# Windowed attention and two expert layers on one core: order and buffers of the first loads, casts of the weights

## The chip, the cores and the metric

The kernel runs on one core of one Trainium2 chip. The metric is the device time of an execution in microseconds (us), as the median of several runs. One core has TensorE (PE, which multiplies matrices), VectorE (DVE), ScalarE (ACT), GpSimd (POOL) and SyncE (SP); here SyncE issues all the transfers between HBM and the core's SBUF. Matrix products are written to PSUM, which has eight banks here, shared out over three rings.

## The reference

```python
# q, k, v: (4, 8, 576, 64)
scores = (q @ k.transpose(0, 1, 3, 2)) / sqrt(64)
rel = pos[:, None] - pos[None, :]
scores = where((rel >= 0) & (rel < 64), scores, -1e9)
attn = exp(scores - max(scores)); attn /= sum(attn) + 1e-9
x = (attn @ v)                       # to (2304 tokens, 512)
h = maximum(x @ w_in, 0);  x = (h * h) @ w_out          # d_ff = 2048
h = x @ w2_in;             out = (h * cos(h)) @ w2_out  # d_ff = 2048
```

The weights reach the kernel as 64-bit floating point numbers, read as pairs of 32-bit words, and are converted on the chip. Products are made in float32 split into a high and a low part (three products for one).

## The kernel before

**Staging.** The 2304 tokens are cut into nine attention units n of 256 tokens, each in two groups g of heads. `attention(n, g, key, sp, ...)` loads qk (576 KB) and v (512 KB), makes the scores S on TensorE (`scores`, L451), takes the masked maximum on VectorE (`neg_max`, L463), the exponential on ScalarE (`exp`, L469), sums and normalises on VectorE (L475 to L479), transposes on TensorE (T, L487), copies the result to PT, multiplies by v on TensorE (O, L501), and writes the high part of X on ScalarE (L535) and the low part on VectorE (L538). Scores, T and O of a group pass through one ring of PSUM banks: "acc" (four banks) for group (0,0), "at" (two banks) for all others. qk, v, pb and PT have one buffer each for all the groups.

**Weights.** w1 has 16 blocks j. `convert_w` loads the raw words of a block (1024 KB, L271) into one of 17 weight buffers "W", scales both words on ScalarE (L241, two instructions), shifts, merges and adds on VectorE (L294, L297, L302), casts the result to the high part in a second buffer (`c5`, L241 on ScalarE or L245 on VectorE) and subtracts for the low part (L323, VectorE). The raw buffer is free after that. The load of block j waits for the low part of block j - 4. Blocks of w2 are converted in the same way later and stored to HBM.

**Products.** `units` are UnitA (first layer; units 0, 1 and 2 of 256 tokens, then pairs of 512) and UnitB (second layer, 384 tokens). `items` is the list of (unit, j) in TensorE's order. For each item `g1` makes the first product ph (12 matmuls, L814), ScalarE and VectorE make g from it (L578 to L591), and `g2` makes the second product accA (12 matmuls, L605) LAG = 2 items later. g1 and g2 are tied in a line by `line`. Unit 0 is alone for the first SK = 4 blocks; then its items alternate with those of unit 1:

```python
SK = 4
items = [(units[0], j) for j in range(SK)]
for j in range(NJ - SK):
    items += [(units[0], SK + j), (units[1], j)]
```

**Order.** Every step is an `op` with the engines that may do it and a cost for each, a key, what it depends on, and the buffers it takes and uses. `Plan.run` walks through time: of the ops that can start within 0.03 us of the earliest it takes the one with the lowest key, on the engine that would end it first. What comes out is a fixed order on each engine; on the chip each engine takes its instructions in that order and waits for what each needs. A transfer costs SyncE 0.6 us in the plan and lands 1.6 us plus its bytes at 250 GB/s later. The first calls are

```python
for g in range(NG):
    attention(0, g, -60.0 + 8.0 * g, 4.0)
for j in range(NJ):
    convert_w(w1, j, (-12.0) + 3.0 * (j if j < SK else 2 * j - SK),
              w_lo[j - 4][1] if j >= 4 else None, early=(-60.0) + 4.0 * j if j < 3 else None)
```

Of the kernel before, what the change touches and what calls it, by code (L numbers as in the profile page):

```python
# [85 lines left out]
class Plan:  # L86
# [6 lines left out]
    def op(self, engs, key, fn, deps=(), take=(), use=(), lat=None):  # L93
        if lat is None:
            lat = self.PE_LAT if "PE" in engs else self.LAT
        o = Op(engs, key, fn, [d for d in deps if d is not None], list(take), lat)
        o.seq = len(self.ops)
        self.ops.append(o)
        for b in (*take, *use):
            b.users.append(o)  # L100
        return o
# [61 lines left out]
def act_us(n, sbuf=True):  # L163
    return 0.05 + 0.093 * sbuf + n / 1200.0
# [15 lines left out]
def kernel(  # L180
# [24 lines left out]
    NUA = NT // UA  # L205
    NUB = NT // UB
    HB = UA // P
    LAG = 2

    psum = bass.MemoryType.PSUM  # L210
# [20 lines left out]
    X = cp.tile([P, 2, NCC, 4 * UA], F32R, name="X")  # L231

    def dma(key, fn, nbytes, deps=(), take=(), use=(), n=1, order=()):
        return op({"SP": 0.6 * n}, key, fn, [*deps, *order], take, use, lat=1.6 + nbytes / 250e3)

    def eng_of(e):
        return {"DVE": nc.vector, "POOL": nc.gpsimd}[e]
# [22 lines left out]
    def convert_w(src, j, key, after=None, dst=None, early=None):  # L260

        nm = f"{src.tensor.name}_{j}"
        raw, rb = {}, R["W"].buf()
        wb = R["W"].buf() if dst is None else None

        def ld(e):
            raw["t"] = wp.tile([P, 2, DM, 2], I32, tag=f"W{rb.slot}", name=f"raw_{nm}")  # L270
            nc.sync.dma_start(  # L271
                raw["t"].rearrange("p a n two -> p (a n two)"), src[j].bitcast(I32))

        o_ld = dma(key - 3 if early is None else early, ld, P * 2 * DM * 8, [after], [rb])

        def words():
            t = raw["t"].rearrange("p a n two -> p (a n) two")
            return t[:, :, 0], t[:, :, 1]

        def c0(e):  # L280
            hw = words()[1].bitcast(F32)
            copy(e, hw, hw, 2.0**-112)

        def c1(e):
            lw = words()[0]
            copy(e, lw, lw.bitcast(U32), 2.0**-29)

        o0 = op({"ACT": act_us(2 * DM)}, key, c0, [o_ld], use=[rb])
        o1 = op({"ACT": act_us(2 * DM)}, key, c1, [o_ld], use=[rb])
        s, tb = {}, R["w"].buf()  # L290

        def c2(e):
            s["w"] = cv.tile([P, 2 * DM], I32, tag="w", name=f"cw_{nm}")
            nc.vector.tensor_scalar(s["w"], words()[1], 3, None, ALU.logical_shift_left)  # L294

        def c3(e):
            nc.vector.scalar_tensor_tensor(  # L297
                s["w"], words()[1], -(1 << 31), s["w"], ALU.bitwise_and, ALU.bitwise_or)

        def c4(e):  # L300
            w = words()[1] if dst is None else s["w"]
            nc.vector.tensor_tensor(w, s["w"], words()[0], ALU.add)  # L302

        def w32():
            if dst is None:
                return raw["t"].bitcast(F32)[:, :, :, 1]
            return s["w"].bitcast(F32).rearrange("p (a n) -> p a n", a=2)

        o2 = op({"DVE": dve_us(2 * DM, True)}, key, c2, [o0], [tb], use=[rb])
        o3 = op({"DVE": dve_us(2 * DM)}, key, c3, [o2], use=[rb, tb])  # L310
        o4 = op({"DVE": dve_us(2 * DM) + 0.3}, key, c4, [o3, o1], use=[rb, tb])
        if dst is None:
            tb = rb
        if dst is not None:
            return [dma(key, lambda e: nc.sync.dma_start(dst[j], w32()), P * 2 * DM * 4, [o4],
                        use=[tb])]

        def c5(e):
            new_w(wb, nm)
            copy(e, wb.tile[:, :, 0], w32())  # L320

        def c6(e):
            nc.vector.tensor_tensor(  # L323
                wb.tile[:, :, 1], w32(), f32(wb.tile[:, :, 0]), ALU.subtract)

        hi = op({"ACT": act_us(2 * DM), "DVE": dve_us(2 * DM, True) + 0.3}, key, c5, [o4],
                [wb], [tb])
        lo = op({"DVE": dve_us(2 * DM)}, key, c6, [hi], use=[tb, wb])
        w_hi[j] = [hi, hi]
        w_lo[j] = [lo, lo]  # L330
        w_buf[j] = wb
# [75 lines left out]

    x_hi = {}
    x_lo = {}
    loads = []  # L410
    turns = {"acc": None, "at": None}

    spans = [(0, 1), (1, 1), (2, 1)] + [(n, 2) for n in range(3, NUA, 2)]
    x_col = [0, UA, 2 * UA] + [((n - 3) % 4) * UA for n in range(3, NUA)]
# [1 line left out]
        [m for m in range(n) if x_col[m] == x_col[n]][-1:] for n in range(NUA)]  # L416
    g1_last = {}

    def attention(n, g, key, sp):

        nm = f"{n}_{g}"
        t = {}
        ring = "acc" if n == 0 and g == 0 else "at"
        pool = ps_acc if ring == "acc" else ps_at
        qb, vb, pbuf, smb, ptb = (R[x].buf() for x in ("qk", "v", "pb", "sm", "PT"))
        sb = [R[ring].buf() for _ in range(2)]
        tb = [R[ring].buf() for _ in range(2)]
        ob = R[ring].buf()

        def load_qk(e):  # L430
            t["qk"] = ap_.tile([P, 2, QK], F32, tag="qk", name=f"qk_{nm}")
            nc.sync.dma_start(t["qk"], qk[n, g])

        def load_v(e):
            t["v"] = ap_.tile([P, NR, 4, D], F32, tag="v", name=f"v_{nm}")
            nc.sync.dma_start(t["v"], v[n, g])

        l0 = dma(key - 3, load_qk, P * 2 * QK * 4, [], [qb], order=loads[-1:])
        l1 = dma(key - 2, load_v, P * NR * 4 * D * 4, [], [vb], order=[l0])
        loads.append(l1)  # L440

        def scores(eng):
            t["pb"] = ap_.tile([P, 2, 2, HB, P], F32, tag="pb", name=f"pb_{nm}")
            S = t["S"] = [
                pool.tile([P, 2, HB, P], F32, tag=ring, name=f"S_{nm}_{e}") for e in range(2)]
            for r in range(2):
                for i in range(HB):
                    for e in range(2):
                        for c in range(2):
                            q0 = (2 * i + c) * WINDOW  # L450
                            nc.tensor.matmul(  # L451
                                S[e][HALF[c], r, i], t["qk"][HALF[e], r, q0:q0 + WINDOW],
                                t["qk"][HALF[e], r, UA + q0:UA + q0 + P],
                                start=(r == 0 and i == 0), stop=(r == 1 and i == HB - 1),
                                skip_group_check=True)

        o_s = op({"PE": 0.35 + 8 * 0.104}, key, scores, [l0, turns[ring]], [*sb, pbuf], [qb])

        def neg_max(eng, e, r, i):
            if e == 0 and r == 0 and i == 0:  # L460
# [27 lines left out]

        def p_copy(eng, e):
            if e == 0:  # L490
                t["pt"] = ap_.tile([P, 2, 2, UA], F32, tag="PT", name=f"PT_{nm}")
            copy(eng, t["pt"][:, e].rearrange("p r q -> p (r q)"),
                 t["T", e].rearrange("p r i q -> p (r i q)"))

# [13 lines left out]
        for e in range(2):  # L508
            k_e = key + e * sp
            ex = []  # L510
            for r in range(2):
                for i in range(HB):
                    first = prev is None
                    prev = op({"DVE": 0.36}, k_e, lambda q, e=e, r=r, i=i: neg_max(q, e, r, i),
                              [o_s, o_mask[mask_kind(HB * n + i)], prev],
                              [smb] if first else [],
                              [sb[e], pbuf] + ([] if first else [smb]))
                    ex.append(op({"ACT": 0.59}, k_e, lambda q, e=e, r=r, i=i: exp(q, e, r, i),
                                 [prev], use=[pbuf, smb]))
            o_r = op({"DVE": 0.33}, k_e, lambda q, e=e: recip(q, e), ex, use=[smb])  # L520
            o_n = op({"DVE": dve_us(512)}, k_e, lambda q, e=e: norm(q, e), [o_r], use=[smb, pbuf])
            o_t = op({"PE": 4 * pe_us(P)}, k_e, lambda q, e=e: transp(q, e),
                     [o_n, o_setup], [tb[e]], [pbuf])
            o_pt = op({"ACT": act_us(512, False), "DVE": dve_us(512)}, k_e,
                      lambda q, e=e: p_copy(q, e), [o_t, o_pt],
                      [] if e else [ptb], [tb[e]] + ([ptb] if e else []))
            o_p.append(o_pt)
        o_v = op({"PE": 0.35 + 16 * 0.053}, key + sp, weighted, [l1, *o_p], [ob], [ptb, vb])
        turns[ring] = o_v
# [250 lines left out]

    units = [UnitA(n, k) for n, k in spans] + [UnitB(n) for n in range(NUB)]
    NSA = len(spans)
    SK = 4
    items = [(units[0], j) for j in range(SK)]
    for j in range(NJ - SK):
        items += [(units[0], SK + j), (units[1], j)]
# [57 lines left out]

    cv = ctx.enter_context(tc.tile_pool(name="cv", bufs=1))
    for g in range(NG):
        attention(0, g, -60.0 + 8.0 * g, 4.0)
    for j in range(NJ):
        convert_w(w1, j, (-12.0) + 3.0 * (j if j < SK else 2 * j - SK), w_lo[j - 4][1] if j >= 4 else None, early=(-60.0) + 4.0 * j if j < 3 else None)
    w2_done = {}  # L850
    gs = {}

    def att_key(n, g):
        if n == 1:
            return -40.0 + 8.0 * g, 4.0
        if n <= 4:
            return 16.0 + 8.0 * (n - 2) + 4.0 * g, 2.0
        s = 3 + (n - 5) // 2
        return s * NJ + 6.0 * ((n - 5) % 2) + 3.0 * g, 1.5
# [97 lines left out]
```

## Time and profile before

| what | value |
|---|---|
| median of 3 runs | 917.96 us (915.41 to 918.77) |
| profiled execution | 918.24 us |
| its span, first to last instruction | 916.4 us |
| mean granted TensorE clock | 0.989 |
| busy: PE, DVE, ACT | 881.4, 570.4, 469.1 us |

The profile shows one execution. A row of the timeline gives start, duration, engine, source line, operation, output and inputs and the number of instructions merged, and in brackets how long the engine stood idle before it and who ended that. Busy shares of TensorE say that it has work, not that it works at its peak: at a granted clock of 0.5 the same matmuls take twice as long.

### The profile page before, as it was taken

How to read it: one execution, taken by the hardware profiler on the slowest of the kernel's cores; microseconds unless marked ns; L12 is line 12 of the kernel's file. 1: busy time of each engine (PE TensorE's matmuls, PEld its weight loads, DVE VectorE, ACT ScalarE, POOL GpSimd, SP SyncE). 2: the span in 40 equal slices, each digit the busy share in tenths (PEclk: the TensorE clock that was granted, in tenths of full speed). 3: DMA queues.
4: the chain of work that ended last, by engine and by line, in shares of the span. 5: the costliest groups of instructions: out<-in, count | busy, mean ns of one | idle time of the engine just before them, and what ended most of it. 6: DMA issues, size and time to landing. Idle time of an engine off the chain costs nothing.

```text
span 916.4 us, 14455 instructions
## 1 busy us (share of the span) xinstructions
PE 881.4 (96%) x5616; PEld 777.3 (85%) x5616; DVE 570.4 (62%) x1307; ACT 469.1 (51%) x1007; POOL 5.0 (1%) x25
## 2 busy tenths in 40 slices
PE   3689899999999999999999999999999999999998
PEld 2579899998888878887888999898989999898987
DVE  4999886544544355534444976766766766866664
ACT  5878757666655566644433543433443433433433
POOL 2000000000000000000000000000000000000000
PEclk9799999999999999999999999999999999999999
DMA  6565315433444254323342200200200200200000
GB/s 266 228 221 218 131 61 167 163 122 119 153 153 141 70 187 156 127 95 124 124 175 92 73 9 1 66 5 1 69 1 1 70 1 1 70 1 1 35 1 35
DMA packets 23749, 85.47 MB, mean 93 GB/s; under 512 B 2433, under 2 KB 7041, under 8 KB 19585
## 3 DMA queue, kind: packets, MB, share of 16 engines
q1 hardware_dynamic: 23680, 84.55, 26.4%
q8 instruction: 44, 0.72, 0.3%
q14 instruction: 25, 0.20, 0.1%
HBM read 66.72 MB, written 17.83 MB: 92 GB/s over the span
## 4 chain that ended last, share of the span: by engine, by line
PE 92%; DVE 3%; DMA 2%; ACT 1%; issue 1%; ACTq 0%; DVEq 0%
PE ph L814 44%; PE accB L747 22%; PE accA L605 21%; PE S L451 2%; PE O L501 2%; DMA qk<-in_qk_dram 2%; PE T L487 1%; DMA x_dram<-x 1%; DVE W_in_w_dram L323 1%; DVE cw_in_w_dram L297 1%; DVE cw_in_w_dram L294 0%; DVE pb L479 0%; DVE X L538 0%; ACT g L582 0%; ACT r L586 0%
## 5 line engine op out<-in xcount | busy, mean ns | idle before, releaser
L814 PE MATMUL ph<-X,W_in_w_dram 128*128 128x256 f32 (+1 forms) x1152 | 225.4, 344 | 5.0 <-DVE W_in_w_dram L323 3.4
L605 PE MATMUL accA<-g,W_in_w_dram 128*128 128x256 f32 (+1 forms) x1152 | 223.2, 340 | 2.0 <-ACT x L625 1.6
L814 PE MATMUL ph<-X,W 128*128 128x384 f32 x1152 | 218.0, 337 | 0.0
L747 PE MATMUL accB<-W,gb 128*128 128x512 f32 x864 | 216.4, 395 | 0.0
L814 PEld LDWEIGHTS ph<-X,W 128*128 128x128 f32 x1152 | 205.2, 188 | 8.6
L814 PEld LDWEIGHTS ph<-X,W_in_w_dram 128*128 128x128 f32 x1152 | 182.8, 193 | 31.5 <-DVE W_in_w_dram L323 4.0
L605 PEld LDWEIGHTS accA<-g,W_in_w_dram 128*128 128x128 f32 x1152 | 180.5, 191 | 25.8 <-ACT x L625 2.5
L747 PEld LDWEIGHTS accB<-W,gb 128*128 128x128 f32 x864 | 161.0, 188 | 30.5
L698 ACT ACTIVATE u<-ph,quarter 128x384 f32<-128x384 f32 x96 | 55.7, 581 | 151.4 <-PE ph L814 151.4
L591 DVE TENSOR_TENSOR g<-r,g 128x256 fp32r<-128x256 f32 (+1 forms) x96 | 53.3, 556 | 103.0 <-ACT r L586 102.2
L702 DVE TENSOR_SCALAR u<-u 128x384 f32<-128x384 f32 x96 | 34.5, 359 | 109.4 <-ACT u L698 109.4
L582 ACT ACTIVATE g<-r 128x256 fp32r<-128x256 f32 (+1 forms) x96 | 50.3, 524 | 97.8 <-PE accA L605 96.4
L724 ACT ACTIVATE gb<-rr 128x384 fp32r<-128x384 f32 x96 | 50.5, 526 | 87.5 <-DVE rr L720 86.8
L578 ACT ACTIVATE r<-ph 128x256 f32<-128x256 f32 (+1 forms) x96 | 46.6, 486 | 55.3 <-PE ph L814 54.4
L241 ACT ACTIVATE raw_in_w_dram<-raw_in_w_dram 128x1024 f32<-128x1024 f32 x64 | 71.5, 1148 | 1.4 <-DMA raw_in_w_dram<-in_w_dram 1.4
L469 ACT ACTIVATE pb<-pb,mm 128x128 f32<-128x128 f32 x144 | 55.9, 391 | 11.2 <-DVE mm L463 11.2
L717 ACT ACTIVATE u<-rr,hpi 128x384 f32<-128x384 f32 x96 | 58.5, 609 | 0.3 <-DVE rr L713 0.3
L720 DVE TENSOR_TENSOR rr<-ph,u 128x384 f32<-128x384 f32 x96 | 52.9, 551 | 4.7 <-ACT u L717 4.7
L706 DVE SCALAR_TENSOR_TENSOR rr<-u,ph 128x384 f32<-128x384 f32 x96 | 53.1, 553 | 3.0
L727 DVE TENSOR_TENSOR gb<-rr,gb 128x384 fp32r<-128x384 f32 x96 | 53.0, 552 | 0.6 <-ACT gb L724 0.6
L710 DVE SCALAR_TENSOR_TENSOR rr<-u,rr 128x384 f32<-128x384 f32 x96 | 52.8, 550 | 0.6
L586 ACT ACTIVATE r<-r 128x256 f32<-128x256 f32 (+1 forms) x94 | 49.1, 523 | 2.9
(58 smaller groups left out, 540.4 us busy)
## 6 DMA issues: line engine op xcount, KB each, us to landing
raw_in_w_dram<-in_w_dram SPq DMA_DIRECT2D x32, 1024.0 KB, 6.3
qk<-in_qk_dram SPq DMA_DIRECT2D x18, 576.0 KB, 4.0
v<-in_v_dram SPq DMA_DIRECT2D x18, 512.0 KB, 3.7
w_dram<-cw_in_w_dram SPq DMA_DIRECT2D x16, 512.0 KB, 3.0
w<-w_dram SPq DMA_DIRECT2D x8, 1024.0 KB, 4.9
x_dram<-x SPq DMA_DIRECT2D x18, 256.0 KB, 2.2
xr<-x_dram SPq DMA_DIRECT2D x24, 192.0 KB, 2.4
out_dram<-o SPq DMA_DIRECT2D x18, 256.0 KB, 2.1
```

Of the source, the lines that this page charges most:

```text
L241: nc.scalar.activation(o, i, AF.Copy, scale=scale)
L469: nc.scalar.activation(t["pb"][:, e, r, i], t["pb"][:, e, r, i], AF.Exp, bias=t["mm"][:, e, r, i:i + 1], scale=-1.0, accum_out=t["sm"][:, ...
L591: nc.vector.tensor_tensor(t["g"][:, 1], t["r"], f32(t["g"][:, 0]), ALU.subtract)
L605: nc.tensor.matmul(self.acc[i][:, k, :], w[:, 1, wl, m * P:m * P + P], t["g"][:, gl, :], start=(j == 0 and p == 0 and k == 0), stop=(j == ...
L698: nc.scalar.activation(t["u"], ph()[:, 0:UB], AF.Identity, bias=quarter, scale=INV_2PI)
L706: nc.vector.scalar_tensor_tensor(t["r"], t["u"], -C1, ph()[:, 0:UB], ALU.mult, ALU.add)
L710: nc.vector.scalar_tensor_tensor(t["r"], t["u"], -C2, t["r"], ALU.mult, ALU.add)
L717: nc.scalar.activation(t["u"], t["r"], AF.Sin, bias=hpi)
L720: nc.vector.tensor_tensor(t["r"], ph()[:, 0:UB], t["u"], ALU.mult)
L727: nc.vector.tensor_tensor(t["g"][:, 1], t["r"], f32(t["g"][:, 0]), ALU.subtract)
L747: nc.tensor.matmul(self.acc[m], t["g"][:, gl, m * P:m * P + P], w[:, 1, wl], start=(j == 0 and k == 0), stop=(j == NJ - 1 and k == 2))
L814: nc.tensor.matmul(t["ph"][:, 0:u.w], wb.tile[:, 0, wl, c * P:c * P + P], u.x(xl, c), start=(c == 0 and k == 0), stop=(c == NCC - 1 and k ...
```

## The change

At the beginning the loads of qk of both groups of unit 0 get the lowest keys (-99, -98), ahead of the first weight blocks (-96, -94.5), and v of both groups -97 and -95.5. The dependency that put each group's load behind the loads of the group before (`loads`) is removed. The second groups of units 0 and 1 (`guest`) take three of the weight buffers in place of the single qk, v, pb and PT buffers, through a helper `room`, and group (0,1) uses the two banks of the "ph" ring. SK becomes 2, and the keys of the weight conversions change. `c5`, the cast of a weight block's high part, is allowed on ScalarE alone. In the planner a transfer now occupies SyncE for its bytes at 360 GB/s (at least 0.6 us) and lands 2.2 us after that, and an extra 0.3 us on `c4` is dropped.

```diff
+    A0, A1 = 2.0, -40.0
     def dma(key, fn, nbytes, deps=(), take=(), use=(), n=1, order=()):
-        return op({"SP": 0.6 * n}, key, fn, [*deps, *order], take, use, lat=1.6 + nbytes / 250e3)
+        return op({"SP": max(0.6 * n, nbytes / 360e3)}, key, fn, [*deps, *order], take, use, lat=2.2)
...
-        o4 = op({"DVE": dve_us(2 * DM) + 0.3}, key, c4, [o3, o1], use=[rb, tb])
+        o4 = op({"DVE": dve_us(2 * DM)}, key, c4, [o3, o1], use=[rb, tb])
...
-        hi = op({"ACT": act_us(2 * DM), "DVE": dve_us(2 * DM, True) + 0.3}, key, c5, [o4],
-                [wb], [tb])
+        hi = op({"ACT": act_us(2 * DM)}, key, c5, [o4], [wb], [tb])
...
-    loads = []
-    turns = {"acc": None, "at": None}
+    turns = {"acc": None, "ph": None, "at": None}
...
-    def attention(n, g, key, sp):
+    def attention(n, g, key, sp, early=None):
...
-        ring = "acc" if n == 0 and g == 0 else "at"
-        pool = ps_acc if ring == "acc" else ps_at
-        qb, vb, pbuf, smb, ptb = (R[x].buf() for x in ("qk", "v", "pb", "sm", "PT"))
+        ring = {(0, 0): "acc", (0, 1): "ph"}.get((n, g), "at")
+        pool = {"acc": ps_acc, "ph": ps_ph, "at": ps_at}[ring]
+        smb = R["sm"].buf()
+
+        guest = n < 2 and g == 1
+        if guest:
+            qb, vb, ptb = (R["W"].buf() for _ in range(3))
+            pbuf = ptb
+        else:
+            qb, vb, pbuf, ptb = (R[x].buf() for x in ("qk", "v", "pb", "PT"))
+
+        def room(name, buf, at, shape):
+            if not guest:
+                return ap_.tile([P, *shape], F32, tag=name, name=f"{name}_{nm}")
+            if at == 0:
+                t[buf] = wp.tile([P, 4 * DM], F32, tag=f"W{buf.slot}", name=f"{name}_{nm}")
+            size = math.prod(shape)
+            flat = t[buf][:, at:at + size]
+            dims = " ".join("abcd"[:len(shape)])
+            return flat.rearrange(
+                f"p ({dims}) -> p {dims}", **dict(zip("abcd", shape)))
...
-        l0 = dma(key - 3, load_qk, P * 2 * QK * 4, [], [qb], order=loads[-1:])
-        l1 = dma(key - 2, load_v, P * NR * 4 * D * 4, [], [vb], order=[l0])
-        loads.append(l1)
+        k_qk, k_v = early or (key - 3, key - 2)
+        l0 = dma(k_qk, load_qk, P * 2 * QK * 4, [], [qb])
+        l1 = dma(k_v, load_v, P * NR * 4 * D * 4, [], [vb], order=[l0])
...
-                      [] if e else [ptb], [tb[e]] + ([ptb] if e else []))
+                      [] if e or guest else [ptb],
+                      [tb[e]] + ([ptb] if e or guest else []))
...
-    SK = 4
+    SK = 2
...
-        attention(0, g, -60.0 + 8.0 * g, 4.0)
+        attention(0, g, -60.0 + A0 * g, 4.0, (-99.0 + g, -97.0 + 1.5 * g))
...
-        convert_w(w1, j, (-12.0) + 3.0 * (j if j < SK else 2 * j - SK), w_lo[j - 4][1] if j >= 4 else None, early=(-60.0) + 4.0 * j if j < 3 else None)
+        convert_w(w1, j, -6.0 + 2.0 * (j if j < SK else 2 * j - SK), w_lo[j - 4][1] if j >= 4 else None, early=-96.0 + 1.5 * j if j < 2 else None)
...
-            return -40.0 + 8.0 * g, 4.0
+            return A1 + 8.0 * g, 4.0
```

The tiles of qk, v, pb and PT are made by `room` in the places where `ap_.tile` made them.

## Rows read from the trace of the kernel before

**Rows 1.** The page's first part: busy us, share of the span, instructions.

```profile
PE 881.4 (96%) x5616; PEld 777.3 (85%) x5616; DVE 570.4 (62%) x1307; ACT 469.1 (51%) x1007; POOL 5.0 (1%) x25
```

**Rows 2.** Busy time of each engine by stretch; then granted clock, DMA share, GB/s.

```profile
0.00:21.50 21.50, 7.85 (x104) 6.24 (x104) 8.66 (x36) 10.70 (x25) 4.99 (x25) 1.00 0.69 275
21.50:60.10 38.60, 28.00 (x280) 23.79 (x281) 35.33 (x88) 31.41 (x82) 0.00 (x0) 0.82 0.56 210
60.10:125.00 64.90, 59.55 (x562) 57.38 (x561) 59.03 (x108) 49.09 (x109) 0.00 (x0) 0.97 0.44 165
125.00:420.00 295.00, 295.00 (x2285) 254.33 (x2285) 148.11 (x405) 179.42 (x436) 0.00 (x0) 1.00 0.39 132
420.00:436.00 16.00, 14.09 (x54) 10.63 (x53) 4.93 (x8) 5.54 (x10) 0.00 (x0) 0.89 0.47 173
```

**Rows 3.** SyncE's queue, timeline of its first issues.

```profile
0.73 0.37 SPq L432 DMA_DIRECT2D qk<-in_qk_dram  x1
1.16 2.18 SPq L271 DMA_DIRECT2D raw_in_w_dram<-in_w_dram  x4
3.38 0.47 SPq L436 DMA_DIRECT2D v<-in_v_dram  x1
6.63 0.33 SPq L432 DMA_DIRECT2D qk<-in_qk_dram  x1
```

**Rows 4.** The chain that ended last, first 125 us: start, us, what.

```profile
0.73 3.79 DMA qk<-in_qk_dram
...
6.63 10.51 DMA qk<-in_qk_dram
...
67.33 1.44 PE accA L605 x12
```

**Rows 5.** TensorE's timeline, parts of the first 62 us.

```profile
17.19 1.99 PE L451 MATMUL S<-qk 64*64 64x128 f32 x32 [3.15 <-DMA qk<-in_qk_dram]
19.10 1.78 PE L501 MATMUL O<-PT,v 128*64 128x64 f32 x32
...
33.53 1.97 PE L451 MATMUL S<-qk 64*64 64x128 f32 x28 [1.01 <-DVE X L538]
35.42 4.43 PE L814 MATMUL ph<-X,W_in_w_dram 128*128 128x256 f32 x27
...
46.60 1.09 PE L451 MATMUL S<-qk 64*64 64x128 f32 x28 [1.05 <-DVE X L538]
...
60.11 1.60 PE L814 MATMUL ph<-X,W_in_w_dram 128*128 128x256 f32 x12
```

**Rows 6.** VectorE's timeline, the X subtractions of groups (1,0) and (1,1).

```profile
45.85 0.69 DVE L538 TENSOR_TENSOR X<-O,X 128x512 fp32r<-128x512 f32 x1
...
58.66 0.69 DVE L538 TENSOR_TENSOR X<-O,X 128x512 fp32r<-128x512 f32 x1 [1.05 <-ACT X L535]
```

**Rows 7.** Groups of instructions from 60.1 to 125, shapes apart: busy us, mean ns.

```profile
L297 DVE SCALAR_TENSOR_TENSOR cw_in_w_dram<-raw_in_w_dram,cw_in_w_dram 128x1024 int32<-128x1024 int32 x10 | 12.2, 1225 | 0.3
L302 DVE CUSTOM_DVE_ANT_0 raw_in_w_dram<-raw_in_w_dram,cw_in_w_dram 128x2048 uint16<-128x2048 uint16 x10 | 12.2, 1222 | 0.1
L323 DVE TENSOR_TENSOR W_in_w_dram<-raw_in_w_dram,W_in_w_dram 128x1024 fp32r<-128x1024 f32 x9 | 11.0, 1221 | 0.3 <-ACT W_in_w_dram L241 0.2
...
L591 DVE TENSOR_TENSOR g<-r,g 128x256 fp32r<-128x256 f32 x17 | 7.2, 422 | 4.4 <-ACT r L586 4.3
...
L294 DVE TENSOR_SCALAR cw_in_w_dram<-raw_in_w_dram 128x1024 int32<-128x1024 int32 x9 | 6.2, 688 | 0.0
L245 DVE CAST W_in_w_dram<-raw_in_w_dram 128x1024 fp32r<-128x1024 f32 x6 | 4.2, 693 | 0.2
L241 ACT ACTIVATE W_in_w_dram<-raw_in_w_dram 128x1024 fp32r<-128x1024 f32 x3 | 3.5, 1158 | 1.3 <-DVE raw_in_w_dram L302 1.3
```

**Rows 8.** Who made TensorE wait after 125 us: in total, times, longest.

```profile
PE accA L605 <- ACT x L625: 1.6, 2, 0.9
```

**Rows 9.** Who made VectorE wait in the first 66 us.

```profile
DVE pb L463 <- PE S L451: 9.9, 2, 6.7
```

More of the change, by code (lines that the diff above doesn't have):

```diff
@@ L430, in load_qk @@
         def load_qk(e):
-            t["qk"] = ap_.tile([P, 2, QK], F32, tag="qk", name=f"qk_{nm}")
+            t["qk"] = room("qk", qb, 0, [2, QK])
             nc.sync.dma_start(t["qk"], qk[n, g])
         def load_v(e):
-            t["v"] = ap_.tile([P, NR, 4, D], F32, tag="v", name=f"v_{nm}")
+            t["v"] = room("v", vb, 0, [NR, 4, D])
             nc.sync.dma_start(t["v"], v[n, g])
-        l0 = dma(key - 3, load_qk, P * 2 * QK * 4, [], [qb], order=loads[-1:])
-        l1 = dma(key - 2, load_v, P * NR * 4 * D * 4, [], [vb], order=[l0])
-        loads.append(l1)
+        k_qk, k_v = early or (key - 3, key - 2)
+        l0 = dma(k_qk, load_qk, P * 2 * QK * 4, [], [qb])
+        l1 = dma(k_v, load_v, P * NR * 4 * D * 4, [], [vb], order=[l0])
         def scores(eng):
-            t["pb"] = ap_.tile([P, 2, 2, HB, P], F32, tag="pb", name=f"pb_{nm}")
+            t["pb"] = room("pb", pbuf, 0, [2, 2, HB, P])
             S = t["S"] = [
@@ L455, in scores @@
                                 skip_group_check=True)
-        o_s = op({"PE": 0.35 + 8 * 0.104}, key, scores, [l0, turns[ring]], [*sb, pbuf], [qb])
+        o_s = op({"PE": 0.35 + 8 * 0.104}, key, scores,
+                 [l0, turns[ring]], [*sb, pbuf], [qb])
         def neg_max(eng, e, r, i):
@@ L490, in p_copy @@
             if e == 0:
-                t["pt"] = ap_.tile([P, 2, 2, UA], F32, tag="PT", name=f"PT_{nm}")
+                t["pt"] = room("PT", ptb, 2 * DM, [2, 2, UA])
             copy(eng, t["pt"][:, e].rearrange("p r q -> p (r q)"),
```

## The prediction

> **What bounds the kernel now.** I read the page's busy shares first: TensorE (PE) has work 96% of the span [rows 1]. That is an average, so I cut the span into stretches [rows 2]. The reader is to see that TensorE's idle time lies at the beginning: 13.65 us before 21.5 (21.50 - 7.85), 10.6 from 21.5 to 60.1 (38.60 - 28.00), 5.35 from 60.1 to 125; none from 125 to 420 and 1.91 from 420 to 436. In the second stretch the granted clock is also 0.82 on average, so part of the work between 21.5 and 60.1 ran at 1.2 instead of 2.4 GHz. What can be won lies before 125; from there to 420 TensorE is full, and work shifted there comes out one for one at the end.
>
> Second view, SyncE's queue and the chain of waits: qk of group (0,0) is issued at 0.73, then four weight blocks, then v of (0,0), and only at 6.63 qk of group (0,1), because the one qk buffer is read until then [rows 3]. It lands 10.51 us later, at 17.14 [rows 4], since 4 x 1024 + 512 KB lie ahead of it: from 4.52, when the first qk landed, 5184 KB took 12.62 us, 421 GB/s. TensorE takes its work in order, so O of (0,0) at 19.10 stands behind S of (0,1) at 17.19 [rows 5].
>
> Third view, TensorE's timeline: the groups come one at a time. S of (1,0) starts in earnest at 33.53, S of (1,1) at 46.60 [rows 5], each after the X subtraction of the group before (45.85 for (1,0)) has freed its bank; the last, of (1,1), runs at 58.66 [rows 6], and at 60.11 the first product of unit 1 starts [rows 5]. From there TensorE alternates units 0 and 1 and is 92% busy. So my landmark is the start of that product. By the order of items and LAG = 2, five first products (items 0 to 4) and three second ones are behind it.
>
> **The change part by part.** *Loads.* By the keys I work out this order on SyncE: qk(0,0), qk(0,1), W0, v(0,0), v(0,1), W1, qk(1,0), qk(1,1), W2, then v of unit 1 and W3. The planner's costs serve me only for order. qk(0,1) then lands at 4.52 + 0.590 MB / 421 GB/s = 5.9 instead of 17.14, before S of (0,0) is through at 6.6 (from 4.56, 2.0 us long at this clock like the S at 17.19 [rows 5]). qk(1,0) has 576 + 1024 + 512 + 512 + 1024 + its own 576 KB behind the first: 4.325 MB / 421 GB/s = 10.3, so 14.8. The price is paid by the weights: W1 lands at about 13, W2 at 19, W3 behind v(1,0), which waits for O of (0,0) at 17 to 19 and holds W3 with it, at about 24. VectorE cannot use them sooner, so I cost this at nothing; without that cover it would be the 1024 KB of one block, 2.5 us.
>
> *Buffers.* Groups (0,1) and (1,1) each take three weight buffers of 17, six in all. Until the landmark W0 to W2 and up to four raw blocks are alive, 13 together: no wait. (0,1) takes the two "ph" banks, which nobody uses before the first product: no wait either, but the first product now waits until O(0,1) or T have left them; that was so by data anyway.
>
> *The landmark.* S(1,0) can start at 14.9. From S to the X subtraction's end (1,0) took 13.0 us (33.53 to 46.54) and (1,1) 12.75 (46.60 to 59.35) [rows 5, 6]. That gives 14.9 + 13.0 + 12.75 = 40.7 as the low bound. High bound: if S(1,0) is put behind O(0,1), at about 22, it is 47.8. I take 42.5, near the low end, with 1.8 us because (1,0) now shares ScalarE and VectorE with (0,1). A wait is added here: S(1,0) waits for its qk at 14.8, and O(0,0), ready soon after, stands behind it on TensorE for up to 2 us. X of unit 0 is then complete at about 23 to 24 and W0 about the same time; before, the rest of the first product began at 35.42 [rows 5].
>
> Check by VectorE's work. Up to 60.1 it was busy 8.66 + 35.33 = 44.0 us [rows 2]. At the new landmark only W0 to W2 are needed: two blocks less, 2 x (0.69 + 1.23 + 1.22 + 1.22) = 8.7; the shift of W5, already done, 0.7; the casts of three blocks, 2.1; three subtractions of g, 1.3 [rows 7]. There remain 31.2 us, which from its first instruction at 6.7 [rows 9] end at 42.5 with 87% busy; it ran at 92% from 21.5 to 60.1.
>
> *SK 4 to 2.* Unit 1's first product is item 3 instead of item 5. At the landmark TensorE will have done three first products and one second one, not five and three: four groups of 12 matmuls, 1.44 us each [rows 4], are still owed, 5.8 us. In return every weight block feeds 5.76 us of TensorE work from then on (four groups), against 4.4 us of VectorE conversion.
>
> So the landmark gains 60.1 - 42.5 - 5.8 = 11.8 us; with the bounds 13.6 and 6.5.
>
> *Casts.* From 60.1 to 125 six of nine casts were on VectorE, 0.693 each, three on ScalarE, 1.158 [rows 7]. All on ScalarE: VectorE 59.03 - 4.2 = 54.9 us, ScalarE 49.09 + 6.9 = 56.0 [rows 2, 7]. The busier of the two falls from 59.0 to 56.0, of 64.9. I let this stretch last as long as before; it cannot go below TensorE's 59.55 less about 1.9 for the clock (a mean of 0.97 is some 3.9 us at half rate), so up to 7.3 us may be won; what may be lost is the first rival's price.
> The Trainium skill (Perfetto Trace Analysis, Optimizing Scalar/DVE Operations) says that where VectorE has a faster mode it beats ScalarE, but that offloading can pay when VectorE is saturated. The rows agree on the first half (0.693 against 1.158) and VectorE is 91% busy there; by the first half alone each of the six casts would lose 0.46 us, 2.8 in all.
>
> *The planner's new load costs* (transfer time on SyncE) and the dropped 0.3 us reorder later work too. TensorE is full from 125 to 420, so I cost that at nothing. The exposed place is the 1.9 us of idle time from 420 to 436 [rows 2], most of it TensorE waiting for ScalarE's copies of accA [rows 8]; that wait could go or double: 2 us either way.
>
> **Sum.** The profiled execution took 918.24 (span 916.4 and 1.84 around it), 0.3 above the median of the runs, 917.96. 918.24 - 11.8 = 906.4, by the median 906.2.
>
> **The rivals.** *ScalarE becomes the bound.* For it: 56.0 us must fit where TensorE needs 59, and ScalarE also holds the relus that free TensorE's banks. From 21.5 to 60.1 it reached 31.41 of 38.6, 81%; if its waits keep it at 78%, the stretch takes 56.0 / 0.78 = 71.8, 6.9 more: 913. Against it: six casts are moved, not the whole block.
> *TensorE runs full after the landmark.* Each block now feeds both units from the third on, so conversion gets ahead and the 5.35 us of idle time go: about 900.
> *It does not bring unit 1 earlier*, because VectorE and ScalarE were the limit and not the queue. Then only the casts count, up to 3 us: 915 to 918. Against it: VectorE stood idle 9.9 us for S in this time, the first 6.7 among them [rows 9].
> *Slower.* SK = 2 puts unit 1's first product third in TensorE's order. If group (1,1) is not ready, nothing behind it runs, though W3 and W4 are there. The point is 60.1 - 5.8 = 54.3: an X(1,1) later than that loses, and at the old 59.35 it costs the whole 5.8 us, 924. It would take S(1,0) starting at 28 or later.
>
> **How the numbers follow.** Forecast 0.58, ScalarE 0.15, fuller TensorE 0.12, no earlier 0.07, slower 0.08. The forecast's own range is 903 to 912. The range 899.5 to 914.5 reaches to the fuller TensorE at one end and the ScalarE bound at the other, and leaves the last two out. A measurement here tells about 0.5%, 4.6 us, from no change: faster is the forecast, the third case and about half of ScalarE's, 0.77; within, the rest of that and most of "no earlier", 0.14; slower 0.09.
>
> **What would show it.** qk(0,1) landing near 6 and qk(1,0) near 15; S(1,0) near 15; the rest of the first product near 24; unit 1's first product near 42.5 with W3 just done; no cast of weights on VectorE; ScalarE's busy time in the next 65 us near 56; TensorE full about 12 us earlier, and nothing but that shift afterwards. It is wrong if S(1,0) stands behind O(0,1), if the product of unit 1 waits past 48, if conversions come slower than one in 5.8 us, or if the wait at 420 grows.

## The result and the profile after

The changed kernel takes 904.34 us (median of 4 runs, 903.26 to 905.20) against 918.28 before on the same chip: a ratio of 0.9855, 95% interval 0.9838 to 0.9873, 13.9 us less. The profiled execution took 904.37 with a span of 902.6.

First the stretches of [rows 2] in the changed kernel, same columns:

```profile
0.00:21.50 21.50, 11.58 (x146) 9.50 (x146) 9.39 (x56) 12.09 (x41) 5.03 (x25) 1.00 0.83 330
21.50:60.10 38.60, 29.82 (x297) 26.34 (x296) 36.86 (x71) 33.38 (x69) 0.00 (x0) 0.82 0.57 228
60.10:125.00 64.90, 63.76 (x597) 62.91 (x596) 58.10 (x108) 58.99 (x126) 0.00 (x0) 1.00 0.34 129
125.00:420.00 295.00, 294.72 (x2236) 251.40 (x2235) 143.97 (x402) 179.40 (x432) 0.00 (x0) 1.00 0.42 143
420.00:436.00 16.00, 16.00 (x72) 13.27 (x71) 5.42 (x7) 5.89 (x10) 0.00 (x0) 1.00 0.39 131
```

TensorE idles 9.9 us before 21.5 (13.65 before), 8.8 up to 60.1 (10.6), and only 1.1 up to 125 (5.35), at the full clock. The idle time at 420 to 436 is gone. Before 21.5 the granted clock reads 1.00, but the matmuls don't bear it out: 32 of S take 1.99 us there and 1.10 at 53.12, where the clock is full.

The timeline of SyncE's queue at the beginning, for [rows 3], and then of TensorE, for [rows 5]:

```profile
0.73 0.84 SPq L449 DMA_DIRECT2D qk<-in_qk_dram  x2
1.63 0.42 SPq L272 DMA_DIRECT2D raw_in_w_dram<-in_w_dram  x1
2.09 1.01 SPq L453 DMA_DIRECT2D v<-in_v_dram  x2
3.15 0.57 SPq L272 DMA_DIRECT2D raw_in_w_dram<-in_w_dram  x1
6.78 0.80 SPq L449 DMA_DIRECT2D qk<-in_qk_dram  x2
7.62 0.45 SPq L272 DMA_DIRECT2D raw_in_w_dram<-in_w_dram  x1
8.12 12.94 SPq L453 DMA_DIRECT2D v<-in_v_dram  x2
21.10 0.43 SPq L272 DMA_DIRECT2D raw_in_w_dram<-in_w_dram  x1
```

```profile
4.71 3.69 PE L468 MATMUL S<-qk 64*64 64x128 f32 x64 [4.71 <-DMA qk<-in_qk_dram]
...
15.79 1.08 PE L505 MATMUL T<-ident,pb 128*128 128x128 f32 x4 [2.30 <-ACT pb L487]
16.80 1.99 PE L468 MATMUL S<-qk 64*64 64x128 f32 x32
18.72 1.97 PE L519 MATMUL O<-PT,v 128*64 128x64 f32 x32
...
27.95 1.08 PE L505 MATMUL T<-ident,pb 128*128 128x128 f32 x4 [2.85 <-DVE pb L497]
...
33.97 1.99 PE L468 MATMUL S<-qk 64*64 64x128 f32 x32
...
46.18 2.70 PE L833 MATMUL ph<-X,W_in_w_dram 128*128 128x256 f32 x12
48.71 1.60 PE L624 MATMUL accA<-g,W_in_w_dram 128*128 128x256 f32 x12
50.15 1.60 PE L833 MATMUL ph<-X,W_in_w_dram 128*128 128x256 f32 x12
```

The loads are issued in the forecast order, and TensorE waits for none but the first: S of (0,0) and (0,1) are one run of 64. S of (1,0) starts at 16.8, S of (1,1) only at 33.97, and unit 1's first product, the landmark, at 50.15, behind three first products and one second.

To see where the 13.9 us lie, the start of the same matmul is compared in both timelines (before, then after): the first product of the sixth and last unit of layer one, and the last second products of the kernel:

```profile
412.24 2.88 PE L814 MATMUL ph<-X,W_in_w_dram 128*128 128x512 f32 x12
...
904.37 8.56 PE L747 MATMUL accB<-W,gb 128*128 128x512 f32 x36
```

```profile
402.30 2.88 PE L833 MATMUL ph<-X,W_in_w_dram 128*128 128x512 f32 x12
...
890.51 8.56 PE L766 MATMUL accB<-W,gb 128*128 128x512 f32 x36
```

9.94 us are won by 412, and 13.86 at the end. The other 3.92 are the stall at 420 to 436 [rows 8]: 1.91 of idle time and the slow clock behind it (0.89 on average there, 1.00 in the changed kernel).

### The profile page after: what moved, and what is told of

It is laid out like the page before. It is cut to its first block, busy times and chain, and to the rows that moved or that the text cites. A ratio compares the mean times of both kernels' runs of the same rounds, so it can differ in the third digit from the quotient of the medians.

```text
span 902.6 us, 14462 instructions
## 1 busy us (share of the span) xinstructions
PE 879.0 (97%) x5616; PEld 776.9 (86%) x5616; DVE 563.3 (62%) x1295; ACT 480.2 (53%) x1019; POOL 5.0 (1%) x25
## 4 chain that ended last, share of the span: by engine, by line
PE 91%; ACT 4%; DVE 3%; issue 1%; DMA 0%; ACTq 0%; DVEq 0%
PE ph L833 43%; PE accB L766 22%; PE accA L624 20%; PE S L468 2%; PE O L519 2%; PE T L505 2%; ACT raw_in_w_dram L242 1%; DVE cw_in_w_dram L298 1%; ACT pb L487 1%; DVE pb L481 0%; ACT g L601 0%; DVE pb L497 0%; ACT W_in_w_dram L242 0%; DMA qk<-in_qk_dram 0%; DVE W_in_w_dram L324 0%
```

## The experiments

Times are medians, each with its ratio to the kernel before measured on the same chip. Two theories are told apart. A: the early part gains because the groups, and unit 1 above all, are ready earlier. B (called C when narrowed): it gains because the blocks are converted faster than TensorE uses them up. The first runs undo one part of the changed kernel; those with one part alone put it into the kernel before.

### Undoing one part of the changed kernel

**SK.**

```diff
-    SK = 2
+    SK = 4
```

> The changed kernel with SK = 4 again (the keys of the conversions follow SK by their formula). Theory A (the early part gains because unit 1's groups are ready earlier, whatever the item order): unit 1 is ready at the same 48.6 us, at most 2 us slower, 904 to 906.5. Theory B (it gains because each converted block then feeds two units, so that TensorE no longer waits for weights after 60 us): TensorE has to wait for W3 (53.6 in the changed kernel) before unit 1 may start, and idle time comes back between 50 and 125: 4 to 8 us slower, 908 to 912. The late part (no stall at 420) should stay as in the changed kernel by both.

906.65 us, ratio 0.9890 (0.9875 to 0.9906), 0.0035 above the changed kernel's, about 3 us. It lies between the two expectations. TensorE idles 1.7 us from 60.1 to 125 instead of 1.1, so few of the waits of theory B come back. SK = 2 is a small part.

**Casts.**

```diff
-        hi = op({"ACT": act_us(2 * DM)}, key, c5, [o4], [wb], [tb])
+        hi = op({"ACT": act_us(2 * DM), "DVE": dve_us(2 * DM, True) + 0.3}, key, c5, [o4],
+                [wb], [tb])
```

> The changed kernel with the cast of a block's high part on ScalarE or VectorE again. Theory A (readiness of unit 1): within 1.5 us of the changed kernel, 903 to 906. Theory B with the casts as part of it (VectorE paces the conversions): VectorE takes some nine casts of 0.69 us back, the last block's conversion ends 3 to 6 us later than at 115.4, and 2 to 4 us of TensorE's waits return: 906 to 908.5. If ScalarE is the tighter engine in the changed kernel, it is faster by 1 to 3 us.

911.11 us, ratio 0.9938 (0.9920 to 0.9956), 0.0083 or 7.6 us worse: more than either theory said. VectorE's timeline has the last step of W5 and W15, with the cast of W15:

```profile
61.55 1.23 DVE L324 TENSOR_TENSOR W_in_w_dram<-raw_in_w_dram,W_in_w_dram 128x1024 fp32r<-128x1024 f32 x1
...
137.60 0.69 DVE L246 CAST W_in_w_dram<-raw_in_w_dram 128x1024 fp32r<-128x1024 f32 x1
138.33 1.23 DVE L324 TENSOR_TENSOR W_in_w_dram<-raw_in_w_dram,W_in_w_dram 128x1024 fp32r<-128x1024 f32 x1
```

The last block is ready at 139.6, and TensorE stands for it, after a wait for a step of attention (2.63):

```profile
134.47 0.63 PE L506 MATMUL T<-ident,pb 128*128 128x128 f32 x4 [2.63 <-DVE pb L498]
135.81 1.15 PE L520 MATMUL O<-PT,v 128*64 128x64 f32 x30 [0.46 <-ACT PT L242]
138.35 0.51 PE L834 MATMUL ph<-X,W_in_w_dram 128*128 128x256 f32 x2 [1.39 <-DVE W_in_w_dram L246]
139.61 1.72 PE L834 MATMUL ph<-X,W_in_w_dram 128*128 128x256 f32 x9 [0.76 <-DVE W_in_w_dram L324]
```

**The planner's cost of a transfer.**

```diff
-        return op({"SP": max(0.6 * n, nbytes / 360e3)}, key, fn, [*deps, *order], take, use, lat=2.2)
+        return op({"SP": 0.6 * n}, key, fn, [*deps, *order], take, use, lat=1.6 + nbytes / 250e3)
```

> The changed kernel with the planner's old cost of a transfer (0.6 us of SyncE, then 1.6 us and 250 GB/s). If the new cost is what took away the stall at 420 to 436, the stall is back and the run is 3.9 us slower, 908; if the stall went because the shift of the beginning changed the meeting of copies and transfers by chance, it stays away or comes in another size: 904 to 906. The early part should hold within 1.5 us by both, since all the first loads are issued within the first 10 us anyway.

908.96 us, ratio 0.9914 (0.9899 to 0.9930), 0.0059 or 5 us worse. The stall is back; the waits of TensorE from 400 to 440 have one row:

```profile
PE accA L624 <- ACT x L644: 1.4, 2, 0.7
```

Its clock stays at 1.00 this time, and by the profiles the late part loses 2.0 us, not 3.9. The early part loses 2.7 us as well, which was not expected: with the old cost more weights go ahead of qk of (1,0), TensorE waits 4.42 us for it, and S of (1,0) starts at 21.4, not 16.8.

**Borrowed buffers and ph banks.**

```diff
-        ring = {(0, 0): "acc", (0, 1): "ph"}.get((n, g), "at")
+        ring = {(0, 0): "acc"}.get((n, g), "at")
...
-        guest = n < 2 and g == 1
+        guest = False
```

> The changed kernel with one qk, v, pb and PT buffer for all groups and group (0,1) on the two banks of all others, so that qk(0,1) waits for S(0,0) again; keys, SK, casts and costs as changed. Theory A: X of (1,1) slips back to about 59 us, the first product of unit 1 to 60, and the run is 6 to 8 us slower, 910 to 912.5. Theory B: the blocks are converted while the groups wait, TensorE finds more of them ready, and it is 0 to 3 us slower, 904 to 907.5.

911.39 us, ratio 0.9943 (0.9930 to 0.9957), 0.0088 or 8 us worse: theory A by its number. W3 is ready at 44.3, but item 3 in TensorE's order is unit 1's first product. Its first half runs at 43.95 with X of (1,0); the second half (57.70 and 58.64) waits for X of (1,1), and everything behind it with it:

```profile
50.20 1.09 PE L505 MATMUL T<-ident,pb 128*128 128x128 f32 x4 [5.27 <-DVE pb L497]
...
58.64 1.43 PE L833 MATMUL ph<-X,W_in_w_dram 128*128 128x256 f32 x5 [0.36 <-DVE X L557]
59.87 2.76 PE L624 MATMUL accA<-g,W_in_w_dram 128*128 128x256 f32 x12
62.43 1.97 PE L833 MATMUL ph<-X,W_in_w_dram 128*128 128x256 f32 x12
```

So this run alone would make the buffers the largest part. The runs from the other side say otherwise.

### One part alone in the kernel before

**Casts on ScalarE** (the opposite of the diff of the casts).

> The kernel before with one edit: casts of the weights on ScalarE alone. Theory 1 (VectorE paces the conversions in the kernel before, so each cast taken from it counts by itself): the last block's conversion ends 4 to 8 us before 132.6 and the run is 3 to 6 us faster, 912 to 915. Theory 2 (the casts count only together with earlier groups, because before the limit was the queue of groups): within 1.5 us of the kernel before, 916 to 919.

908.64 us, ratio 0.9909 (0.9895 to 0.9924), 8.6 us faster: theory 1, beyond its range. S of (0,1) is at 17.4; unit 1's first product has its first half at 58.8 and its second, with X of (1,1), at 62.6, no earlier than before. The conversions run faster. By the profiles the early part wins 6.5 us; another 1.7 lie at 420 to 436, where TensorE still waits 1.6 us, but its clock stays at 1.00. The last step of W5 and of W15 in this run, and then in the kernel before:

```profile
63.62 1.22 DVE L323 TENSOR_TENSOR W_in_w_dram<-raw_in_w_dram,W_in_w_dram 128x1024 fp32r<-128x1024 f32 x1
...
117.70 1.22 DVE L323 TENSOR_TENSOR W_in_w_dram<-raw_in_w_dram,W_in_w_dram 128x1024 fp32r<-128x1024 f32 x1
```

```profile
64.60 1.22 DVE L323 TENSOR_TENSOR W_in_w_dram<-raw_in_w_dram,W_in_w_dram 128x1024 fp32r<-128x1024 f32 x1
...
131.35 1.22 DVE L323 TENSOR_TENSOR W_in_w_dram<-raw_in_w_dram,W_in_w_dram 128x1024 fp32r<-128x1024 f32 x1
```

Ten blocks take 54.1 us, 5.41 each; before they took 66.75, 6.68 each. TensorE's four groups for a block take 5.76. The edit also moves other work in the planned order: X of (2,0), done at 88.9 before, now comes at 111.3, so half of unit 2's attention leaves this stretch.

**The planner's cost of a transfer** (the opposite of the diff of the cost).

> The kernel before with one edit: the planner's new cost of a transfer. If the new cost by itself keeps the weights' transfers out of the way of the copies of accA, the stall at 420 to 436 goes: 3 to 4 us faster, 914 to 915.5, with the beginning unchanged within 1.5 us. If the stall is a matter of how that place happens to meet, it stays: 917 to 919.5.

907.46 us, ratio 0.9890 (0.9875 to 0.9905), 9.8 us faster. The stall is gone as expected, but the beginning wins up to 8.0 us too, which no expectation held. (The 8.0 are from the profiles, which differ by 12.0 us in all: this one is the fastest of its four runs, at 906.23.) With weights that occupy SyncE in the plan, qk of (0,1) moves ahead of two of them: S of (0,1) starts at 14.1 instead of 17.2. That is 3 us, but only 0.8 are left of them at X of (1,1) (58.6 instead of 59.4). The blocks keep theirs: W5 is ready at 61.9, 3.9 us earlier, and ten blocks then take 62.6 us instead of 66.75 (W15 at 124.5), with 8 casts on VectorE instead of 10. Which reordered step brings what isn't separated.

**A later load of x**, so that the two buffers that it shares with the copies of accA are free at 421.

```diff
-            loaded = units[NSA].load(pos - 6, [])
+            loaded = units[NSA].load(pos - 6, [late])
...
+        if i == NA - 8:
+            late = line[0]
```

> The kernel before with one edit: the first load of x for the second layer waits for the product eight items ahead of the second layer instead of being issued as soon as its buffers allow, so that the two buffers it shares with the copies of accA are free at 421. If the stall at 420 to 436 comes from those shared buffers and the transfers queued with that load, it goes and nothing else changes: 914 to 915 (3.9 us off), the beginning as before to 0.1 us. If it comes from the reload of the weights alone, which still stands ahead of the first store, it stays: 918.

914.44 us, ratio 0.9970 (0.9958 to 0.9982), 2.8 us faster, and 3.5 by the profiled spans (912.9 against 916.4). TensorE has no wait from 400 to 440. The stall was the shared buffers with the transfers queued at that moment. The cost of a transfer decides whether they meet: the four runs with the old cost and the early load of x have the stall (1.4 to 1.9 us of idle time), the nine with the new cost at most 0.1 us.

**Casts and planner's cost together.**

> The kernel before with the casts on ScalarE alone and the new cost of a transfer, without the first loads' keys, the borrowed buffers, the ph banks and SK = 2. Alone the two gave 8.6 and 9.8 us. Theory C (conversions pace the beginning, and the earlier groups only matter where they would otherwise come later than the weights): the two together already reach the changed kernel, 902 to 906.5, and the reordering adds at most 2 us to them. Theory A (earlier groups carry their own share): 908 or slower would leave them 4 us; the sum of the two by themselves without overlap, 899, would be a surprise to both.

906.55 us, ratio 0.9875 (0.9855 to 0.9895), at the edge of theory C. The two overlap: alone they gave 0.0091 and 0.0110, together 0.0125, and the changed kernel 0.0145. The intervals of the last two overlap.

**All of the reordering without them**: the changed kernel with the old casts and the old cost.

> The changed kernel with the old casts and the old cost of a transfer: first loads' keys, borrowed buffers, ph banks, SK = 2 and the conversions' keys alone. Theory C: little is left of the early gain, and the stall at 420 may be back: 913 to 918. Theory A: most of the early 9.9 us stays, 906 to 910.

920.24 us, ratio 1.0031 (1.0014 to 1.0048): slower than before. Theory A is out as the main cause. X of (1,1) is ready at 53.7 instead of 59.4, but 14 of 16 casts are on VectorE (10 before), W15 is ready at 147.2 instead of 132.6, and TensorE idles 5.1 us after 125.

With this run all eight combinations of three parts are measured. The reordering holds all that is neither casts nor cost, the dropped 0.3 us on `c4` too:

| casts | cost | without the reordering | with it |
|---|---|---|---|
| old | old | 1 | 1.0031 |
| new | old | 0.9909 | 0.9914 |
| old | new | 0.9890 | 0.9938 |
| new | new | 0.9875 | 0.9855 |

In no row does the reordering gain more than the intervals allow, and without the new casts it costs time.

### Earlier groups, earlier weights

**Group (1,1) on accA's banks.**

```diff
-        ring = {(0, 0): "acc", (0, 1): "ph"}.get((n, g), "at")
+        ring = {(0, 0): "acc", (0, 1): "ph", (1, 1): "acc"}.get((n, g), "at")
```

> The changed kernel with group (1,1) on the four banks of accA, which stand empty from 24 to 48 us, so that its S no longer waits for the X subtraction of (1,0). X of (1,1) should then be there near 40 instead of 48.6. If unit 1's readiness still sets the pace, the run is 4 to 7 us faster, 897 to 900. If the conversions do (W2 46.8, W3 53.6 in the changed kernel), the earlier group only moves VectorE's work about: within 2 us, 902.5 to 906.

903.37 us, ratio 0.9853 (0.9837 to 0.9870), the same as the changed kernel. X of (1,1) is there at 39.6 instead of 48.6, and unit 1's first product still starts at 50.8, since W2 comes at 46.8 as before. In the changed kernel an earlier group buys nothing more.

**First conversions ahead of unit 1's groups.**

```diff
-    A0, A1 = 2.0, -40.0
+    A0, A1 = 2.0, -8.0
```

> The changed kernel with the groups of unit 1 at keys -8 and 0 instead of -40 and -32, so that the first conversions go ahead of them. W0 should be ready near 27 instead of 32.8 and X of (1,1) near 53 to 56 instead of 48.6. Theory C: with SK = 2 the third item still waits for unit 1, so what W0 to W2 win early is taken back in part: within 2 us, 902.5 to 906.5. If the readiness of unit 1 is the tighter one, 3 to 6 us slower, 907.5 to 910.5.

910.71 us, ratio 0.9923 (0.9901 to 0.9944): 6 us slower, at the readiness side. W3 is ready at 45.6, X of (1,1) at 57.3; the second half of unit 1's first product waits for it, at 57.4, and the next first product is at 61.2. Of the 7.5 us that this profile loses by the last unit of layer one, 2.7 are idle time of TensorE; the rest is work at a lower clock, granted 0.63 instead of 0.82 from 21.5 to 60.1. With SK = 2 the group must not come later either.

**Casts on ScalarE or GpSimd**, beside accA's banks for (1,1).

```diff
-        hi = op({"ACT": act_us(2 * DM)}, key, c5, [o4], [wb], [tb])
+        hi = op({"ACT": act_us(2 * DM), "POOL": pool_us(2 * DM)}, key, c5, [o4], [wb], [tb])
```

> The changed kernel with group (1,1) on accA's four banks (903.4 as measured) and, besides, the weights' casts on ScalarE or GpSimd, whichever is free sooner by the plan; VectorE gets none. If ScalarE, which now carries all the casts, is what holds W0 to W4 back (35.7 to 57.5 there), GpSimd takes most of the casts from it and the run is 2 to 4 us faster, 899 to 901.5. If VectorE or the chain of steps of a block sets the pace, it is within 1.5 us, 902 to 905; if GpSimd's cast takes much longer than ScalarE's 1.15 us or slows VectorE down, it is slower than 905.

910.05 us, ratio 0.9925 (0.9911 to 0.9939): 0.0072 or 6.6 us worse than without GpSimd. The groups of GpSimd from 12 to 125, and two of VectorE from 20 to 125, shapes apart; then the same two where ScalarE has all casts:

```profile
L244 POOL TENSOR_SCALAR W_in_w_dram<-raw_in_w_dram 128x1024 fp32r<-128x1024 f32 x13 | 18.5, 1426 | 84.1 <-DVE raw_in_w_dram L303 61.2 <-ACT r L605 6.3 <-issue 4.6
...
L298 DVE SCALAR_TENSOR_TENSOR cw_in_w_dram<-raw_in_w_dram,cw_in_w_dram 128x1024 int32<-128x1024 int32 x16 | 25.3, 1584 | 0.4
...
L295 DVE TENSOR_SCALAR cw_in_w_dram<-raw_in_w_dram 128x1024 int32<-128x1024 int32 x16 | 13.3, 829 | 0.1
```

```profile
L298 DVE SCALAR_TENSOR_TENSOR cw_in_w_dram<-raw_in_w_dram,cw_in_w_dram 128x1024 int32<-128x1024 int32 x16 | 19.6, 1223 | 0.3
...
L295 DVE TENSOR_SCALAR cw_in_w_dram<-raw_in_w_dram 128x1024 int32<-128x1024 int32 x16 | 11.0, 688 | 0.2
```

ScalarE is relieved (49.6 us busy from 60.1 to 125 against 58.3), VectorE is not: 62.8 against 57.5, and TensorE idles 4.2 us there against 0.85. From W5 to W15 VectorE is busy 54.96 of 55.92 us, against 51.02 of 52.48. Here VectorE's time per block counts, not ScalarE's.

## Why the prediction was right, and what in it was not

The sum, 11.8 us, came out as 13.9, inside the forecast's own range, but from other terms: the landmark gave 4.2 us instead of 11.8, the stretch after it 5.7 instead of 0, and the late stall 3.9 instead of 0. That the number fits is luck: two terms entered at nothing made up for one that came to a third. By the prediction's own sign (unit 1's product past 48, at 50.15) its account was wrong. And the edits that it took for the cause, order and buffers of the first loads, are not what makes the kernel faster: casts and cost alone reach 0.9875, and the reordering without them 1.0031.

**Loads: right in order, and not what set the pace.** Every load was there before it was needed. S of (1,0) stood behind T of (0,0) on TensorE, not behind its qk, and O of (0,0) behind S of (1,0), as forecast. In the run with the old cost, where weights go ahead of it, S of (1,0) did wait for its qk.

**The landmark: mis-sized.** 60.11 - 50.15 - 5.76 leaves 4.2. From S of (1,0) to S of (1,1) it took 17.2 us where I had put 13.0 and 1.8 for sharing: VectorE does W0's and W1's steps between the group's, in its planned order, and T at 27.95 waits 2.85 us for its pb, which itself comes after the exponential on ScalarE and a step of W0. W0 came at 32.8, not 24, and W2 at 46.8. My check by VectorE's busy time had the share nearly right, 85% measured against 87%, but not the work: by the landmark VectorE had done 36.73 us, not 31.2, some 3.5 of them for steps of W3 and W4, which I had not counted:

```profile
6.84:50.15 43.31, 29.32 (x304) 24.06 (x297) 36.73 (x115) 35.20 (x93) 0.00 (x0) 0.84 0.69 282
```

The run with accA's banks shows the other half of the error: even a group at 39.6 doesn't move the landmark, because W2 doesn't. I had taken the groups alone as its clock. So the rival "It does not bring unit 1 earlier" came nearer in its mechanism: the engines that make the groups and the blocks were the limit, not the queue. Its price for the casts, up to 3 us, was too small.

**Casts: the step that failed.** I let the stretch after the landmark last as long as before, because the busier of ScalarE and VectorE falls only from 59.0 to 56.0 of 64.9 us. What I did not compare is VectorE's time per block, with all that it does meanwhile, and TensorE's: I wrote 4.4 us against 5.76 and left out the casts, the subtractions of g and unit 2's attention. The stretch from W5 to W15, ten blocks, shows it; before, with the casts alone on ScalarE, and in the changed kernel:

```profile
65.82:132.57 66.75, 62.61 (x565) 60.94 (x566) 60.70 (x111) 49.91 (x111) 0.00 (x0) 0.97 0.38 143
64.84:118.92 54.08, 54.08 (x519) 53.40 (x519) 51.46 (x96) 50.29 (x104) 0.00 (x0) 1.00 0.42 160
64.13:115.40 51.27, 50.13 (x462) 49.49 (x461) 49.76 (x94) 48.89 (x101) 0.00 (x0) 1.00 0.35 129
```

Per block VectorE (the third busy time in a row) was busy 6.07 us before, then 5.15 and 4.98; TensorE (the first), with unit 2's matmuls beside its four groups, 6.26, then 5.41 and 5.01. Before, both were nearly full, each waited for the other in the planned order, and a block took 6.68 us. With less work on VectorE it took 5.41 and 5.13 (W5 ready at 64.13, W15 at 115.40), and TensorE had next to no wait. That is the rival of the fuller TensorE, for another reason than the one I gave it: idle time from 60.1 to 125 fell from 5.35 to 1.14, which is 4.2 of the 5.7 us; the rest is of the size of the clock's part, 0.97 before and 1.00 after. VectorE's share of time, 91%, looked like room; beside a TensorE at 94% in this stretch there was little. How much of it the cast alone does is not shown: of the 9.2 us of VectorE's work that go with the casts alone, the seven casts make about 4.9, and most of the rest is attention of unit 2, which the new order puts later.

**ScalarE as the bound: refuted.** It is busy 59.0 of 64.9 us, more than the 56 reckoned, because more blocks pass in this time (11 last steps, W5 to W15, against 9 [rows 7]), and TensorE waits 1.1 us in all. The Trainium skill's rule (Perfetto Trace Analysis, Optimizing Scalar/DVE Operations) holds here in its second half: the slower cast pays, with VectorE 91% busy. Taken alone, its first half would have given the wrong sign.

**Slower by SK = 2: the mechanism is real.** In two runs X of (1,1) came at 58.6 and 57.3, past the point of 54.3, and the second half of unit 1's first product stood until then; they lost 8 and 6 us against the changed kernel. The borrowed buffers mostly pay for the shorter lead: without SK = 2 and without them, casts and cost alone reach 0.9875.

**The planner's cost: not nothing.** I gave the stall at 420 two us either way; it was worth 3.9 in this profile, with the slow clock behind it, and it follows the cost in both directions (gone alone, back when undone). In the three other runs that have the stall the clock stays at 1.00, and it costs 2.0 to 2.2. The early part of this edit I had not priced at all; alone it gave up to 8.0 us, and S of (0,1) starts 3 us earlier in it.

What stays open: how the early 9.9 us divide among the parts, since they overlap (undone one by one, SK, casts, buffers and banks, and cost lose 2.7, 6.5, 7.6 and 2.7 us of it), and which of the steps moved by the cost or by the casts' edit makes the conversions faster.

## What to carry to other kernels

Where two engines work in turns, lay their times per turn side by side, with everything that each does in it: VectorE's 91% looked like room here, but 6.07 us beside TensorE's 6.26 left none for the waits in between, and a turn took 6.68. With 5.15 beside 5.41 it took 5.41. Take such a time from the busy time of a stretch; single durations added up come out too long, since an instruction can begin before the one ahead of it is over (before, the L323 at 68.05 takes 1.23 us, and the next instruction starts at 69.19). A change that names one thing may gain by another: before crediting the reordering, run it without the edits that came along; here it alone is 0.3% slower. And in a planned order a mere cost in the plan is an edit of the kernel, with effects far from the place it was meant for.

## What the runs showed of the hardware

A cast of 128x1024 took 1.43 us on GpSimd on average (1.11 to 1.70), 1.15 on ScalarE and 0.69 on VectorE. With the casts on GpSimd, two of VectorE's steps became longer, from 1.22 to 1.58 and from 0.69 to 0.83 us on average, so the help took away about half of a microsecond of VectorE per block. The average hides which ones. All seven of the sixteen L298 that met a cast on GpSimd took 2.03 to 2.06 us, and the nine others 1.22; three of the eleven L295 that met one took 1.23 to 1.63. L303 and L324 kept their 1.22, but none of them ran at the same time as such a cast, so they show nothing. One meeting:

```profile
61.03 1.59 POOL L244 TENSOR_SCALAR W_in_w_dram<-raw_in_w_dram 128x1024 fp32r<-128x1024 f32 x1 [4.25 <-ACT r L597]
...
61.65 2.05 DVE L298 SCALAR_TENSOR_TENSOR cw_in_w_dram<-raw_in_w_dram,cw_in_w_dram 128x1024 int32<-128x1024 int32 x1
```

The Trainium skill (SBUF — State Buffer, Terms) says that VectorE and GpSimd share a pair of ports that one holds for a whole instruction while the other is blocked. The rows agree that steps which meet get in each other's way: those L298 lost 0.83 us each.
